# First layer's weights converted two row blocks at a time, with the hand-written order of the first units rearranged

## The chip, the cores and the metric

The kernel runs on one core of a Trainium2 chip. The metric is device time in microseconds (us) of one execution. The engines are PE (matrix multiply), DVE (vector), ACT (scalar activation), POOL (GpSimd) and SP, which only issues transfers here.

## The reference

Sparse attention (a local window of 96 keys and 8 global keys, a bias per head), a feed-forward layer with softmax-weighted units and a layer norm, then a gated feed-forward layer. All is float32; the weights come as 8-byte numbers.

```python
# attention: B, H, S, D = 2, 8, 768, 64
scores = scale * (q @ k.T) + bias            # bias: -slope[h] * distance
scores = where(is_global | is_local, scores, -1e9)
a = exp(scores - max); a = a / (sum(a) + 1e-9)
x = (a @ v) as (1536, 512)
# first layer: w_in 512 x 1024, w_out 1024 x 512
h = x @ w_in
solu = h * softmax(h)
ln = (solu - mean) / sqrt(var + 1e-6) * g_ln
x = ln @ w_out
# second layer: w_gate, w_val 512 x 1536, w_out 1536 x 512
xn = x / rms(x) * rms_g
out = (silu(xn @ w_gate) * (xn @ w_val)) @ w_out
```

## The kernel before

**Units.** The 1536 tokens are 12 units of 128 rows. Units 0 and 1 are the first row blocks of the two batch entries and see 128 keys; the others see 256. A unit's attention is done in halves of four heads: `s_mm` (scores, PE), `s_max` (bias and row maximum, DVE, L278 to L282), `s_exp` (ACT, L289), `s_norm` (reciprocal on DVE, L297 and L298, then four multiplications on POOL, L300), `t_mm` (transposes, PE, L316), `t_evac` (copy out of PSUM, ACT L324 or DVE L326), `attend` (PE, L338). `x_hi` and `x_lo` split the result into two parts for PE (L218 on ACT, L356 on DVE).

**First layer.** `up_mm u half` multiplies x by half of w_in (12 matrix multiplies of 512 columns, L473): eight with the high part of the weights, `win0`, and then four with the low part, `win1`. `up_max`, `so_exp`, `so_mul`, `so_mean`, `so_var` make the softmax-weighted layer norm (DVE and ACT). A PSUM tile `hp` of `up_mm` is free for a later unit when `so_mul` (L505) has read it; there are two such buffers. `ln_t` transposes, `down` multiplies by w_out (L558).

**The weights.** A number of 8 bytes lies in memory as a low and a high word. For each block of 128 rows of w_in or w_out and 512 columns there is a load of 512 KB (`w_load`), a scaled copy of the high word (`w_scale`, one instruction, mostly on ACT), three bit operations on DVE (`w_bits` 0, 1, 2 at L390, L392, L396), the rounded high part (`w_hi`, mostly ACT) and the low part, the difference (`w_lo`: L453 on POOL for w_in, L456 on DVE for w_out). There are 16 blocks: 0 to 3 are the first half of w_in, 4 to 7 the second, 8 to 15 are w_out. The staging tiles `wsh` and `wsl` hold two blocks each, the converted words `wch` and `wcl` four each; a load waits until its place has been converted.

**What sets the order.** The string `START` is a list of steps, read from left to right. Each step puts its instructions at the end of its engine's queue, and each engine works through its queue in order, waiting where data are missing. `START` covers units 0 to 3 wholly, the attention of unit 4, most of that of unit 5, and all 16 weight blocks; its first two lines before the change are

```python
load_n, n_floats, load_qk 0 0, load_qk 0 1, bias_tile 0, bias_tile 1
bias_heads 0 0 4 scalar, bias_heads 0 4 8 gpsimd, s_mm 0 0, s_max 0 0, w_load 0, s_mm 0 1 h
```

Behind it the units 4 to 11 run in a loop (`slot`) in which PE's order is written out and the other engines are ordered by a scheduler; then comes the second layer.

Of the kernel before, what the change touches and what calls it, by code (L numbers as in the profile page):

```python
# [51 lines left out]
t_evac 0 1 1, w_scale 3 scalar, w_hi 1 scalar, w_bits 2 1, t_mm 0 2, w_bits 3 0
t_evac 0 2 1, attend 0 0, t_mm 0 3, t_evac 0 3 1, w_load 4, attend 0 1
w_lo 0 gpsimd, w_load 5, w_bits 2 2, w_hi 2 scalar, w_load 6, attend 0 3
s_max 1 0, attend 0 2, w_bits 3 1, w_lo 1 gpsimd, x_hi 0 scalar, x_lo 0
w_bits 3 2, s_exp 1 0, w_hi 3 scalar, w_lo 2 gpsimd, late_constants, w_load 7
w_scale 4 vector, s_max 1 1, w_bits 4 0, w_lo 3 gpsimd, s_norm 1 0, w_bits 4 1
w_scale 5 scalar, s_exp 1 1, w_scale 6 scalar, up_mm 0 0 d, t_mm 1 1, load_qk 3 0
load_v 1, t_mm 1 0, load_v 2, w_scale 7 scalar, t_evac 1 0 1, w_bits 5 0
w_bits 4 2, w_bits 5 1, bias_heads 1 4 6 scalar, w_hi 4 scalar, t_evac 1 1 1, bias_heads 1 0 2 gpsimd  # L60
w_bits 6 0, bias_heads 1 6 8 scalar, s_norm 1 1, s_mm 2 0, w_bits 7 0, t_mm 1 2
t_evac 1 2 1, w_bits 6 1, attend 1 0, w_bits 5 2, w_bits 7 1, t_mm 1 3
attend 1 1, w_hi 5 scalar, t_evac 1 3 1, w_bits 6 2, w_load 9, w_bits 7 2
w_hi 6 scalar, w_lo 4 gpsimd, s_max 2 0, attend 1 2, up_max 0 0, attend 1 3
w_hi 7 scalar, w_load 8, w_scale 8 vector, load_v 4, s_mm 2 1, w_lo 5 vector
s_exp 2 0, x_hi 1 scalar, w_load 10, s_max 2 1, w_load 11, w_lo 6 gpsimd
w_lo 7 gpsimd, w_scale 9, load_qk 4 0, s_norm 2 0, s_exp 2 1, x_lo 1
w_bits 9 0, up_mm 0 1, load_qk 3 1, up_max 0 1, w_bits 8 0, so_exp 0
w_bits 9 1, s_norm 2 1, so_mul 0 0, w_mul 8 none, w_scale 10 scalar, so_mul 0 1
t_mm 2 0, w_bits 8 1, up_mm 1 0, so_mean 0, w_bits 9 2, w_bits 8 2  # L70
up_max 1 0, load_qk 4 1, t_mm 2 1, up_mm 1 1, t_mm 2 2, up_max 1 1
t_evac 2 1 1, t_evac 2 0 1, w_load 12, so_var 0, w_hi 9 scalar, s_mm 3 0
t_evac 2 2 1, attend 2 0, attend 2 2, w_hi 8 scalar, attend 2 1, so_exp 1
t_mm 2 3, w_mul 11 none, s_max 3 0, s_mm 3 1, w_bits 10 0, s_exp 3 0
w_lo 9 vector, t_evac 2 3 0, attend 2 3, x_hi 2 scalar, w_mul 15 none, w_scale 12 gpsimd
so_mul 1 1, s_norm 3 0, s_max 3 1, w_scale 11 scalar, load_v 3, s_exp 3 1
x_lo 2, t_mm 3 0, w_bits 11 0, so_mul 1 0, w_bits 12 0, so_mean 1
w_mul 9 none, t_mm 3 1, w_bits 10 1, s_norm 3 1, w_bits 10 2, so_var 1
t_evac 3 0 1, up_mm 2 0, w_load 14, w_hi 10 scalar, t_evac 3 1 1, up_mm 2 1
# [990 lines left out]
```

## Time and profile before

| | |
|---|---|
| three runs | 558.94, 559.98, 561.72 us (median 559.98) |
| the profiled execution, its own time | 558.16 us |
| its span, first to last instruction | 556.3 us |
| steps of START | up to about 93 us |
| one unit of the loop behind it | 18.9 us |

The span and the time of the profiled execution differ by 1.9 us, which lie ahead of the first and behind the last instruction. A timeline row gives start and duration; where instructions overlap in an engine's pipeline, the distance between the starts of two neighbours is what one of them costs in a full queue, and that is less than its duration.

### The profile page before, as it was taken

The page shows a single profiled execution, that of the slowest core. Times are in us where ns is not written, and L with a number is a line of the kernel's source. Part 1 is how long each engine was busy: PE and PEld are TensorE (multiplying, and loading weights), DVE is VectorE, ACT ScalarE, POOL GpSimd, SP SyncE. Part 2 cuts the span into 40 slices and gives each one's busy share as a digit, 9 for nine tenths or more (in the row PEclk, how much of TensorE's full clock was granted, in tenths as well). Part 3 has the DMA queues.
Part 4 walks back from the last instruction along what each step waited for, and adds up shares of the span by engine and source line. Part 5 has one row for each costly group of instructions (what it writes and reads, how often), then busy time and mean ns, then how long its engine had stood idle before and what let it go on. Part 6 is the DMA issues. An engine that isn't in the chain of part 4 may idle for free.

```text
span 556.3 us, 7639 instructions
## 1 busy us (share of the span) xinstructions
PE 527.8 (95%) x2736; PEld 424.1 (76%) x2736; DVE 333.4 (60%) x797; ACT 236.6 (43%) x557; POOL 179.0 (32%) x207
## 2 busy tenths in 40 slices
...
GB/s 290 254 240 142 247 31 67 95 95 47 51 94 39 1 76 77 115 113 16 140 148 151 1 0 1 75 151 1 1 0 1 75 151 77 0 77 0 77 0 82
DMA packets 16670, 45.93 MB, mean 83 GB/s; under 512 B 1904, under 2 KB 2928, under 8 KB 16624
## 3 DMA queue, kind: packets, MB, share of 16 engines
...
## 4 chain that ended last, share of the span: by engine, by line
PE 70%; DVE 20%; POOL 4%; ACT 3%; issue 2%; DMA 1%; POOLq 0%; DVEq 0%; ACTq 0%; SPq 0%
PE gv L628 30%; PE op L652 15%; PE yp L558 11%; PE hp L473 8%; DVE p L278 3%; DVE e L505 2%; POOL p L300 2%; PE tp L316 2%; DVE hst L481 2%; DVE wc L392 1%; PE xps L338 1%; DVE wc L390 1%; DVE xlo L356 1%; PE tp L587 1%; DVE llo L224 1%
## 5 line engine op out<-in xcount | busy, mean ns | idle before, releaser
L628 PE MATMUL gv<-xgh,w2hi 128*128 128x512 f32 x288 | 112.2, 390 | 0.0
L628 PE MATMUL gv<-xgl,w2hi 128*128 128x512 f32 x288 | 112.0, 389 | 0.0
L628 PE MATMUL gv<-xgh,w2lo 128*128 128x512 f32 x288 | 112.0, 389 | 0.0
L224 POOL TENSOR_TENSOR alo<-th,ahi 128x512 fp32r<-128x512 f32 x36 | 47.6, 1322 | 169.9 <-ACT ahi L223 169.8
L300 POOL TENSOR_SCALAR p<-p,ast 128x256 f32<-128x256 f32 (+1 forms) x96 | 56.7, 608 | 103.5 <-DVE ast L282 67.5
L615 DVE SCALAR_TENSOR_TENSOR th<-th,gv 128x512 f32<-128x512 f32 x36 | 24.7, 685 | 100.0 <-ACT th L614 99.9
L224 POOL TENSOR_TENSOR w2lo<-wc,w2hi 128x512 fp32r<-128x512 f32 x36 | 49.0, 1366 | 63.3 <-ACT w2hi L223 63.3
L473 PE MATMUL hp<-win,xhi 128*128 128x512 f32 x192 | 66.0, 407 | 0.7 <-ACT xhi L218 0.7
L628 PEld LDWEIGHTS gv<-xgh,w2lo 128*128 128x128 f32 x288 | 54.1, 188 | 11.3
L628 PEld LDWEIGHTS gv<-xgl,w2hi 128*128 128x128 f32 x288 | 54.1, 188 | 11.2
L628 PEld LDWEIGHTS gv<-xgh,w2hi 128*128 128x128 f32 x288 | 54.1, 188 | 11.0
L558 PE MATMUL yp<-wout,lhi 128*128 128x512 f32 x192 | 60.9, 398 | 0.3 <-DVE wout L456 0.3
L652 PE MATMUL op<-w2hi,alo 128*128 128x512 f32 x144 | 56.4, 392 | 2.3 <-POOL alo L224 2.3
L223 ACT ACTIVATE ahi<-th 128x512 fp32r<-128x512 f32 x36 | 22.7, 631 | 82.7 <-DVE th L616 82.7
L652 PE MATMUL op<-w2hi,ahi 128*128 128x512 f32 x144 | 56.2, 391 | 1.4 <-ACT ahi L223 1.4
L614 ACT ACTIVATE th<-gv 128x512 f32<-128x512 f32 x36 | 21.3, 591 | 82.1 <-PE gv L628 82.1
L652 PE MATMUL op<-w2lo,ahi 128*128 128x512 f32 x144 | 56.1, 389 | 0.0
L289 ACT ACTIVATE p<-p,ast 128x256 f32<-128x256 f32 (+1 forms) x96 | 45.9, 480 | 7.2 <-DVE ast L282 4.0
L473 PEld LDWEIGHTS hp<-win,xhi 128*128 128x128 f32 x192 | 37.1, 193 | 9.1 <-ACT xhi L218 1.4
L616 DVE SCALAR_TENSOR_TENSOR th<-th,gv 128x512 f32<-128x512 f32 x36 | 24.6, 684 | 30.1 <-PE gv L628 29.9
L558 PEld LDWEIGHTS yp<-wout,lhi 128*128 128x128 f32 x192 | 34.9, 188 | 7.3 <-DVE wout L456 0.8
L473 PE MATMUL hp<-win,xlo 128*128 128x512 f32 x96 | 38.7, 403 | 0.4 <-DVE xlo L356 0.4
...
## 6 DMA issues: line engine op xcount, KB each, us to landing
...
```

The source lines that it names most:

```text
L223: self.nc.scalar.activation(out=hi, in_=src, func=AF.Copy)
L224: lo_eng.tensor_tensor(lo, src, f32(hi), ALU.subtract)
L278: nc.vector.tensor_tensor_reduce(pt[:, i, 0:W], sp[h2][:, pl, :], bias[:, 4 * hh + i, :], 1.0, -3.0e38, ALU.add, ALU.max, st[:, 0, i:i + 1],)
L289: self.nc.scalar.activation(out=pt[:, i, 0:W], in_=pt[:, i, 0:W], func=AF.Exp, scale=0.125, bias=st[:, 1, i:i + 1], accum_out=st[:, 2, i:i ...
L300: nc.gpsimd.tensor_scalar(pt[:, i, 0:W], pt[:, i, 0:W], st[:, 3, i:i + 1], 0.0, ALU.mult, ALU.add)
L473: nc.tensor.matmul(hp, a[:, k, :], self.win[w][:, k, c], start=(n == 0), stop=(n == len(mms) - 1))
L558: nc.tensor.matmul(yp, a[:, k, :], self.wout[w][:, k, :], start=(k == 0 and n == 0), stop=(k == KF - 1 and n == 2),)
L614: nc.scalar.activation(out=a, in_=g, func=AF.Tanh, scale=0.5)
L615: nc.vector.scalar_tensor_tensor(out=a, in0=a, scalar=1.0, in1=g, op0=ALU.add, op1=ALU.mult)
L616: nc.vector.scalar_tensor_tensor(out=a, in0=a, scalar=0.5, in1=v, op0=ALU.mult, op1=ALU.mult)
L628: nc.tensor.matmul(pp, w[:, c], a[:, k, :], start=(n == 0), stop=(n == 3 * KD - 1))
L652: nc.tensor.matmul(self.ops[t], a[:, c], w[:, c0], start=(first and n == 0), stop=(last and n == 2))
```

## The change

Row blocks are loaded and converted in pairs. There are 8 pairs: 0 and 1 are the first half of w_in, 2 and 3 the second, 4 to 7 are w_out. A load is 1 MB; `w_scale` and the three `w_bits` work on 1024 columns instead of 512; `w_hi` and `w_lo` of w_in take 1024 columns in one instruction, except that `w_lo` on POOL, and both for w_out, are two instructions of 512. A pair fills a whole staging tile. `START` is written anew. In it the bias of heads 4 to 7 of the first kind and of heads 0 and 1 of the second moves from POOL to ACT; `w_lo` of pairs 0, 1 and 3 is on DVE, that of pair 2 on POOL; every `w_scale` and `w_hi` is on ACT; the normalisation of unit 3's second half and `x_hi 4` are on DVE; `t_evac 1 1` is on DVE.

```diff
 START = """\
-bias_heads 0 0 4 scalar, bias_heads 0 4 8 gpsimd, s_mm 0 0, s_max 0 0, w_load 0, s_mm 0 1 h
...
+load_n, n_floats, load_qk 0 0, load_qk 0 1, bias_tile 0, bias_tile 1, bias_heads 0 0 4 scalar, s_mm 0 0
...
-    def s_norm(self, u, hh):
+    def s_norm(self, u, hh, eng="gpsimd"):
...
         for i in range(4):
-            nc.gpsimd.tensor_scalar(
-                pt[:, i, 0:W], pt[:, i, 0:W], st[:, 3, i:i + 1], 0.0, ALU.mult, ALU.add
-            )
+            self.scaled(eng, pt[:, i, 0:W], pt[:, i, 0:W], st[:, 3, i:i + 1])
...
     def w_load(self, n):
...
+        st, w = self.early
+        i = self.n_early
+        self.n_early += 1
+        st, w = st[i % 2], w[i % 4 // 2][:, 2 * (i % 2):2 * (i % 2) + 2]
+        half, k = divmod(2 * n, KD) if n < KD else (0, 2 * (n - KD))
+        name = "w_in" if n < KD else "w_out"
+        src = self.d[name][k * P:(k + 2) * P, 2 * half * CW:2 * (half + 1) * CW]
+        self.nc.sync.dma_start(
+            out=st.rearrange("p a b c -> p a (b c)"), in_=src.rearrange("(a p) f -> p a f", p=P)
+        )
+        self.w1[n] = st, w
...
     def w_hi(self, n, eng="scalar"):
...
+        if n < KD:
+            half, k = divmod(2 * n, KD)
+            out = [t[:, k:k + 2, half * CW:half * CW + CW] for t in self.win]
+            self.scaled(eng, out[0], w, 1.0)
         else:
...
+            for i in range(2):
+                self.scaled(eng, out[0][:, i], w[:, i], self.gln[:, k + i:k + i + 1])
...
     def w_lo(self, n, eng="gpsimd"):
...
+        if n < KD and eng == "vector":
+            self.nc.vector.tensor_tensor(lo, w, f32(hi), ALU.subtract)
+            return
+        for i in range(2):
+            if n < KD:
+                self.nc.gpsimd.tensor_tensor(lo[:, i], w[:, i], f32(hi[:, i]), ALU.subtract)
```

Three places in the queues, with the changed kernel's own line numbers in its rows. The first is DVE's queue around the `x_lo` of unit 0, without which PE can't go beyond the first multiply of `up_mm 0 0`. Before (L392 and L396 are the bit operations of single blocks):

```order
L282 TENSOR_SCALAR ast<-ast 128x4
L392 SCALAR_TENSOR_TENSOR wch<-wsl,wch 128x512
L356 TENSOR_TENSOR xlo<-xps,xhi 128x512
L396 SCALAR_TENSOR_TENSOR wch<-wsl,wch 128x512
L157 MEMSET neghalf 128x1
```

The same place now; L370 and L374 are the bit operations of pair 1, L423 is `w_lo 0`, L334 is `x_lo 0`:

```order
L262 TENSOR_SCALAR ast<-ast 128x4
L135 MEMSET neghalf 128x1
L370 SCALAR_TENSOR_TENSOR wch<-wsl,wch 128x1024
L423 TENSOR_TENSOR win_131<-wch,win_130 128x2x512
L374 SCALAR_TENSOR_TENSOR wch<-wsl,wch 128x1024
L334 TENSOR_TENSOR xlo<-xps,xhi 128x512
```

Between the row maximum of unit 1's first half and `x_lo 0` there stand three instructions of 1024 columns where there was one of 512; the difference `w_lo 0` was on POOL.

The second place is DVE's queue around the reciprocal of unit 4's second half (the second pair of L297 and L298), on which POOL's normalisation and then PE's transposes wait. Before:

```order
L297 TENSOR_SCALAR ast<-ast 128x4
L298 RECIPROCAL ast<-ast 128x4
L481 TENSOR_REDUCE hst<-hp 128x1
L390 TENSOR_SCALAR wcl<-wcl 128x512 x3
L456 SCALAR_TENSOR_TENSOR wout_133<-wch,gln,wout_132 128x512
L481 TENSOR_REDUCE hst<-hp 128x1
L392 SCALAR_TENSOR_TENSOR wcl<-wsl,wcl 128x512
L297 TENSOR_SCALAR ast<-ast 128x4
L298 RECIPROCAL ast<-ast 128x4
L392 SCALAR_TENSOR_TENSOR wcl<-wsl,wcl 128x512
L396 SCALAR_TENSOR_TENSOR wcl<-wsl,wcl 128x512
```

Now (L277 and L278 are the reciprocal, L368 to L374 bit operations, L430 `w_lo 5`, L258 the row maximum of unit 5's first half, which goes on for seven more rows):

```order
L277 TENSOR_SCALAR ast<-ast 128x4
L278 RECIPROCAL ast<-ast 128x4
L456 TENSOR_REDUCE hst<-hp 128x1
L368 TENSOR_SCALAR wcl<-wcl 128x1024 x2
L430 SCALAR_TENSOR_TENSOR wout_133<-wch,gln,wout_132 128x512 x2
L456 TENSOR_REDUCE hst<-hp 128x1
L370 SCALAR_TENSOR_TENSOR wcl<-wsl,wcl 128x1024
L277 TENSOR_SCALAR ast<-ast 128x4
L278 RECIPROCAL ast<-ast 128x4
L374 SCALAR_TENSOR_TENSOR wcl<-wsl,wcl 128x1024
L470 TENSOR_SCALAR hst<-hst 128x1
L258 ISA p,ast<-sA,bias_144 128x256
```

The row maximum of unit 5 has moved up to right behind one bit operation after the reciprocal; before, it stood behind four more weight instructions, two `w_lo` and the six of `check_n`.

The third place is PE's queue at the end of `START`: `up_mm 4 1` (hp) with the last multiplies by the low part of w_out (`wout_133`) in it. Before:

```order
L473 MATMUL hp<-win_130,xhi 128x512
L473 MATMUL hp<-win_130,xlo 128x512
L558 MATMUL yp<-wout_133,lhi 128x512
L558 MATMUL yp<-wout_132,llo 128x512
L473 MATMUL hp<-win_130,xhi 128x512
```

Now:

```order
L448 MATMUL hp<-win_131,xhi 128x512 x3
L533 MATMUL yp<-wout_133,lhi 128x512
L533 MATMUL yp<-wout_132,llo 128x512
L533 MATMUL yp<-wout_132,lhi 128x512
L533 MATMUL yp<-wout_133,lhi 128x512
L533 MATMUL yp<-wout_132,llo 128x512
L448 MATMUL hp<-win_131,xhi 128x512
```

Five multiplies of `down 0 3` instead of two are left for this place, and they stand behind eleven of the twelve multiplies of `up_mm 4 1` instead of behind four.

## Rows read from the trace of the kernel before

**Rows 1.** The page: busy time, share of the span, instructions of each engine.
```profile
PE 527.8 (95%) x2736; PEld 424.1 (76%) x2736; DVE 333.4 (60%) x797; ACT 236.6 (43%) x557; POOL 179.0 (32%) x207
```

**Rows 2.** Busy time by stretch: PE, PEld, DVE, ACT, POOL; then PEclk, DMA share, GB/s.
```profile
7.28:36.60 29.32, 21.76 (x93) 13.19 (x93) 26.02 (x85) 21.29 (x68) 23.58 (x27) 0.88 0.75 255
36.60:92.30 55.70, 51.89 (x342) 39.69 (x342) 53.33 (x172) 42.32 (x113) 22.70 (x33) 1.00 0.46 157
0.00:100.00 100.00, 83.43 (x518) 60.68 (x520) 89.63 (x295) 71.14 (x198) 50.84 (x76) 0.97 0.54 181
106.94:125.84 18.90, 18.76 (x125) 15.06 (x124) 12.34 (x44) 10.56 (x30) 4.81 (x10) 1.00 0.23 70
```

**Rows 3.** What PE waited for from 7 to 102 us.
```profile
PE tp L316 <- POOL p L300: 7.9, 11, 1.8
```

**Rows 4.** Busy time in 0 to 100 us of L390, L392, L396, L282, in turn.
```profile
0.00:100.00 100.00, 6.99 (x16) 0.97 0.54 181
0.00:100.00 100.00, 11.61 (x16) 0.97 0.54 181
0.00:100.00 100.00, 11.93 (x16) 0.97 0.54 181
0.00:100.00 100.00, 4.34 (x13) 0.97 0.54 181
```

**Rows 5.** POOL's busy time in 0 to 100 us, L220 first, then L453 (DVE first).
```profile
0.00:100.00 100.00, 1.23 (x3) 7.68 (x8) 0.97 0.54 181
0.00:100.00 100.00, 0.68 (x1) 9.85 (x7) 0.97 0.54 181
```

**Rows 6.** Timeline of DVE: start, duration; the spacing of starts is the cost.
```profile
48.32 0.08 DVE L278 DVE_READ_ACCUMULATOR2_ANT ast<- 128x1 f32 x1
48.66 0.08 DVE L278 DVE_READ_ACCUMULATOR2_ANT ast<- 128x1 f32 x1
...
49.55 0.42 DVE L390 TENSOR_SCALAR wch<-wch 128x512 uint32<-128x512 uint32 x1
49.88 0.74 DVE L456 SCALAR_TENSOR_TENSOR wout<-wch,gln,wout 128x512 fp32r<-128x512 f32 x1
...
62.39 0.68 DVE L396 SCALAR_TENSOR_TENSOR wch<-wsl,wch 128x512 uint32<-128x512 uint32 x1
62.99 0.68 DVE L392 SCALAR_TENSOR_TENSOR wcl<-wsh,wcl 128x512 uint32<-128x512 uint32 x1
...
85.24 0.75 DVE L514 TENSOR_SCALAR e<-e,hst 128x1024 f32<-128x1024 f32 x1
85.91 0.16 DVE L297 TENSOR_SCALAR ast<-ast 128x4 f32<-128x4 f32 x1
```

**Rows 7.** Timeline of POOL: four normalisations of 256 columns each row.
```profile
52.43 1.84 POOL L300 TENSOR_SCALAR p<-p,ast 128x256 f32<-128x256 f32 x4 [1.94 <-DVE ast L298]
...
75.11 4.01 POOL L300 TENSOR_SCALAR p<-p,ast 128x256 f32<-128x256 f32 x4 [1.34 <-DVE ast L298]
```

**Rows 8.** Timeline of PE at the places that the steps speak of.
```profile
20.47 0.80 PE L473 MATMUL hp<-win,xlo 128*128 128x512 f32 x1
...
36.53 0.50 PE L473 MATMUL hp<-win,xhi 128*128 128x512 f32 x1
...
40.13 0.48 PE L473 MATMUL hp<-win,xhi 128*128 128x512 f32 x1
...
52.96 1.80 PE L316 MATMUL tp<-ident,p 128*128 128x128 f32 x8 [1.02 <-POOL p L300]
...
78.70 1.35 PE L316 MATMUL tp<-ident,p 128*128 128x128 f32 x8 [1.42 <-POOL p L300]
...
94.19 1.09 PE L338 MATMUL xps<-pT,v 128*64 128x128 f32 x16
...
100.95 0.66 PE L587 MATMUL tp<-ident,xn 128*128 128x128 f32 x4 [0.47 <-DVE llo L224]
```

**Rows 9.** PE's clock (the column PEclk) in one stretch, as in rows 2.
```profile
29.30:36.04 6.74, 5.97 (x34) 3.61 (x32) 5.86 (x15) 5.57 (x17) 5.79 (x8) 0.50 0.31 103
```

More of the change, by code (lines that the diff above doesn't have):

```diff
@@ L52 @@
[L52 to L79, printed above, removed]
@@ L80 @@
-w_lo 8 vector, load_qk 5 0, w_mul 13 none, up_max 2 0, t_mm 3 3, t_mm 3 2
-up_max 2 1, t_evac 3 3 1, s_mm 4 0, t_evac 3 2 1, w_bits 11 1, w_mul 10 none
-so_exp 2, attend 3 0, attend 3 2, w_lo 10 vector, attend 3 3, w_bits 11 2
-w_bits 12 1, attend 3 1, s_max 4 0, load_qk 5 1, so_mul 2 1, ln_t 0 0
-x_hi 3 scalar, x_lo 3, w_load 13, ln_t 0 1, w_hi 11 scalar, w_load 15
-w_scale 15 gpsimd, so_mul 2 0, s_mm 4 1, s_max 4 1, w_bits 12 2, s_exp 4 0
-up_mm 3 0, s_norm 4 0, w_scale 13 scalar, up_mm 3 1, up_max 3 0, t_mm 4 0
@@ L87 @@
-w_scale 14 scalar, w_bits 14 0, s_exp 4 1, w_bits 13 0, t_evac 4 0 1, w_bits 15 0
-s_mm 5 0, w_lo 11 vector, up_max 3 1, attend 4 0, t_mm 4 1, w_hi 12 scalar
-w_bits 13 1, s_norm 4 1, down 0 0, w_bits 15 1, t_evac 4 1 1, w_bits 13 2
-w_hi 13 scalar, so_exp 3, attend 4 1, w_bits 15 2, load_v 5, t_mm 4 3
-t_mm 4 2, down 0 1, t_evac 4 2 1, attend 4 2, w_bits 14 1, w_lo 12 vector
-t_evac 4 3 1, w_hi 15 scalar, check_n, s_max 5 0, w_bits 14 2, attend 4 3
-s_mm 5 1, x_hi 4 scalar, w_lo 13 vector, w_hi 14 scalar, x_lo 4, so_mul 3 1
@@ new lines @@
+s_exp 2 0, s_norm 2 0, up_mm 0 1, s_exp 2 1, up_max 0 1, x_lo 1, so_exp 0, w_bits 4 0, s_norm 2 1
+so_mul 0 0, so_mul 0 1, t_mm 2 0, w_bits 4 1, so_mean 0, up_mm 1 0, w_bits 4 2, up_max 1 0, t_mm 2 1
+up_mm 1 1, t_mm 2 2, load_qk 4 1, t_evac 2 0 1, so_var 0, t_evac 2 1 1, s_mm 3 0, up_max 1 1, t_evac 2 2 1
+attend 2 0, load_qk 3 1, attend 2 2, attend 2 1, w_hi 4 scalar, t_mm 2 3, so_exp 1, s_mm 3 1, s_max 3 0
+t_evac 2 3 0, s_exp 3 0, attend 2 3, so_mul 1 1, s_norm 3 0, s_max 3 1, w_scale 5 scalar, load_v 3
```

90 lines of the change are left out of this document (40 added, 50 removed).

## The prediction

> **What bounds the kernel now.** The page comes first: PE is busy for 95% of the span, DVE for 60% [rows 1]. The share of PE is an average over two regimes, so the next view is the busy time by stretch. In the loop behind `START` a unit takes 18.90 us, and PE is busy for 18.76 of them, DVE for 12.34 [rows 2]: there PE is the bound, and a gain on DVE, ACT or POOL is worth nothing. In `START` it is otherwise. From 36.6 to 92.3 us DVE is busy for 53.33 of 55.70 us and PE idle for 3.81; from 7.3 to 36.6 us PE is idle for 7.56 [rows 2]. The list of PE's waits says for what: 7.9 us in 11 waits for POOL's normalisation ahead of the transposes [rows 3]. POOL is slow there because of DVE: four normalisations take 1.84 us beside a row maximum, and 4.01 us beside bit operations [rows 7]. So the change can only act by when PE gets through `START`. All that PE is early or late at `up_mm 4`, some 90 us in, goes to the end unchanged, as the loop has 0.14 us of slack a unit. The most to be had behind 36.6 us is the 3.8 us of PE's idle time there.
>
> **What one wide instruction costs.** The spacing of starts in DVE's full queue is read from [rows 6]. A `tensor_scalar` of 512 columns costs 0.33 us (49.55 to 49.88), one of 1024 columns 0.67 (85.24 to 85.91). A two-input operation of 512 columns costs 0.60 (62.39 to 62.99), a step of the row maximum of 256 columns 0.34 (48.32 to 48.66). So 256 columns more cost 0.26, and the trace has no two-input operation of 1024 columns; I take 0.60 + 2 x 0.26 = 1.12 us. The bounds are 1.20 (twice the narrow one, nothing saved) and 0.67 (if it went like the wide `tensor_scalar`); the two-input rows are the nearer.
>
> **The sum on DVE.** Bits: 16 x (0.33 + 2 x 0.60) = 24.5 us become 8 x (0.67 + 2 x 1.12) = 23.3, so -1.2. Three copies (`w_hi 0`, `w_scale` 4 and 8) leave DVE [rows 5]: -1.0. `w_lo`: three of 1.12 for one of 0.60, +2.8. `t_evac 1 1` of 256 columns +0.3, `x_hi 4` +0.6, four normalisations of 256 columns at half of 0.33 +0.7. Together **+2.2 us**: joining the blocks saves less than what is moved to DVE costs.
>
> Against it stands what POOL no longer takes. Of L220 all 7.68 us go; of L453 9.85 us stay two of seven, so -7.0 [rows 5]; one set of normalisations goes, between 1.84 and 4.01, say 2.5 [rows 7]. That is 17.2 of POOL's 50.84 us [rows 2]. What POOL's presence costs DVE now is the excess of durations over undisturbed ones (0.42 for L390, 0.68 for L392 and L396, 0.16 for four columns [rows 6]): 6.99 - 16 x 0.42 = 0.3; 11.61 + 11.93 - 32 x 0.68 = 1.8; 4.34 - 13 x 0.16 = 2.3 [rows 4]; in all 4.4 us. If a third of it goes with a third of POOL's work: **-1.5 us**. The bounds are 0 (what goes lay where DVE wasn't full) and -4.4. DVE's sum is +0.7, between -2.2 and +2.2.
>
> **Where it meets PE**, followed along the queues with these costs.
>
> *The first unit.* `x_lo 0` now stands behind three instructions of 1.12 us where one of 0.60 stood. It ends at about 21.8 us, and the second multiply of `up_mm 0 0`, now at 20.47 [rows 8], comes 1.3 us later. Further on there is a gain: POOL no longer makes two heads of bias between the normalisations of unit 1, so `s_mm 2 1`, right ahead of `up_mm 0 1`, comes 1.8 us earlier. But the last two multiplies of `up_mm 0 1` need `w_lo 3`, now on DVE behind two row maxima (4 x 0.34 + 0.2 each [rows 6]), till about 37.6; and `x_lo 1` follows it. `up_mm 1 0` starts at 39.9 for 40.13 [rows 8]: **-0.2**. ACT, 71% busy over `START` [rows 2], takes the bias heads, which delays `w_scale 3` but not this chain. SP issues fewer, longer loads; pair 0 is first needed after the first exponentials, by which time its two blocks have landed today as well, so the transfers cost nothing unless a load of 1 MB lands a microsecond later than two halves.
>
> *The middle.* From `s_mm 3 0` to the transposes at 52.96 [rows 8] the chain is row maximum, exponentials, reciprocal, normalisation, and none of it changes: PE's 1.02 us of waiting stays. The few tenths gained are lost again at `x_hi 3`, which now stands on ACT behind two `w_hi` of 512 columns. Zero, give or take 0.5.
>
> *Unit 4.* Between the two reciprocals stand 2 x 0.67 + 2 x 0.66 + 1.12 = 3.8 us of weight work instead of 3 x 0.33 + 0.66 + 0.60 = 2.3, and one operation of 0.60 ahead of the first has gone; the second comes at about 75.6, 0.6 later. POOL then waits out one bit operation of 1.12 us, and runs beside the row maximum of unit 5, at 1.84 / 4 = 0.46 us each [rows 7]: 75.8 + 1.1 + 1.8 = 78.7 instead of 79.1. The transposes end at 78.9, not 79.8: **-0.9**, of the 1.42 us of waiting at 78.70 [rows 8].
>
> *The end of START.* DVE has 17.3 us of work from that reciprocal to the end of `w_lo 7`, where it had 16.6 to the end of the last block. `so_mul 3 0`, which frees the buffer for `up_mm 4 1`, comes at 90.1, so PE, there at 89.1, waits 1.0; then it reaches the late multiplies of `down 0 3` as `w_lo 7` is done (92.3 and 92.9). The attention of unit 5 starts at 94.05 for 94.19 [rows 8]: the 0.9 is given back, **+0.8**. `t_evac 5 3`, behind DVE's longer queue, takes up to 0.3 more ahead of 100.95.
>
> Sum: -0.2 + 0.1 - 0.9 + 0.8 + 0.2 = 0.0 us. On the profiled execution of 558.16 us that is 558.2. The median of the runs is 1.8 us higher, at 559.98; against it I forecast **559.9 us, no change**. What a measurement of this kernel can tell from no change is about 0.5%, 2.8 us.
>
> **The rivals.**
>
> *Faster: POOL's absence is worth more.* If most of the 4.4 us goes, or a two-input operation of 1024 columns is nearer to 0.67, DVE is 2 to 4 us ahead at 90 us, `so_mul 3 0` and `w_lo 7` wait for nobody, and PE keeps the 0.9 and most of the waits at 52.96 and 78.70: -3.5, **556.5 us**. For it: 17 us of POOL gone, two waits of PE that hang on POOL [rows 3]. Against it: the wait at 52.96 is a chain through ACT that the change leaves alone. Chance 0.25.
>
> *Slower: wide bit operations hold POOL back.* Beside operations of 0.60 a normalisation took 1.00 us [rows 7], that is 0.46 and most of a DVE instruction. Beside 1.12 it would take 1.5. It decides at unit 4: if the scores of unit 5 are not there when DVE comes to their row maximum, or POOL falls behind it, all four take 6.0 instead of 4.0, and the transposes end 2.2 later; the same in units 0 and 2 adds 1: +3.2, **563 us**, chance 0.12. The Trainium skill, SBUF — State Buffer, section "Who interferes with whom", says that VectorE in a two-port mode or with two SBUF inputs locks out a GpSimd instruction that reads SBUF for the whole instruction, which speaks against this change. By that rule a normalisation beside a bit operation would be 0.46 + 0.60 = 1.06, which the row's 1.00 bears out, and with one SBUF input, as in the row maximum, nothing, which the 1.84 bears out.
>
> *Slower: the clock.* From 29.30 to 36.04 us PE ran at 0.50 of the granted clock, the 1.2 GHz level [rows 9]; then at 1.00 to the end of `START` [rows 2]. It rose behind a stretch in which PE was busy for 5.97 of 6.74 us. The new order puts gaps of one to two microseconds there (for `x_lo 0`, for pair 3, for `w_lo 3`). If it stays low over `up_mm 0 1` and `1 0`, the 3.6 us from 36.53 to 40.13 [rows 8] count twice; up to 38.2 that is hidden behind `w_lo 3`, and from 44 on it costs 3 us. **563 us**, chance 0.06.
>
> **How the numbers follow.** No change has 0.57; its own range, from the sum's +-2 and the scatter of the three runs, is 557.5 to 562. From 556.5 to 562.8 all but some 0.2 are held. Faster by over 0.5% is the first rival, 0.25; slower the other two, 0.18.
>
> **What would show it.** In the changed profile: two-input operations of 1024 columns spaced at 1.1 us; DVE's busy time up to 100 us within 1.5 of 89.6; POOL's down from 50.8 to 34; PE's second multiply 1 us later than 20.47; the wait near 78.7 halved; a new wait of PE on `so_mul` or `w_lo` near 90; the transposes of xn near 101. I am wrong if `up_mm 1 0` starts more than 2 us off 40.1, if the transposes of unit 4 move by more than 2 us, or if PE's clock rises at another time.

## The result, and the profile after

The changed kernel takes 565.11 us (median of 10 runs, 561.27 to 566.17), the kernel before 559.54 (10 runs, 558.07 to 562.55). The ratio is 1.0089, 95% interval 1.0062 to 1.0116: slower, by 5.6 us between the medians and 5.0 by the ratio, and outside the range that was forecast. The profiled execution took 565.0 us, its span is 563.2.

Busy time of the changed kernel by the stretches of [rows 2] (PE, PEld, DVE, ACT, POOL, granted clock, DMA share, GB/s):

```profile
7.28:36.60 29.32, 19.57 (x91) 12.84 (x92) 24.54 (x72) 20.86 (x59) 12.04 (x18) 0.94 0.74 270
36.60:92.30 55.70, 51.70 (x321) 38.54 (x319) 48.89 (x147) 39.14 (x105) 12.89 (x20) 0.94 0.42 149
0.00:100.00 100.00, 80.62 (x465) 58.56 (x466) 83.55 (x252) 67.06 (x184) 29.39 (x57) 0.95 0.50 177
```

DVE is no longer full: from 36.6 us it is idle for 6.8 us instead of 2.4. PE's clock is 0.94 where it was 1.00. The longer loads cost nothing: no engine waits for a weight block in `START`. PE's rows at the places of [rows 8], of the changed kernel (start, length, and in brackets the wait before and who ended it):

```profile
22.09 0.79 PE L448 MATMUL hp<-win,xlo 128*128 128x512 f32 x1 [1.59 <-DVE xlo L334]
22.68 0.63 PE L448 MATMUL hp<-win,xhi 128*128 128x512 f32 x1
23.11 0.63 PE L448 MATMUL hp<-win,xlo 128*128 128x512 f32 x1
23.53 0.63 PE L448 MATMUL hp<-win,xhi 128*128 128x512 f32 x1
...
35.66 0.70 PE L243 MATMUL sA<-qk 64*128 64x256 f32 x2 [1.95 <-DVE ast L258]
...
37.06 0.64 PE L448 MATMUL hp<-win,xhi 128*128 128x512 f32 x1
37.50 0.63 PE L448 MATMUL hp<-win,xlo 128*128 128x512 f32 x1
...
55.82 1.80 PE L294 MATMUL tp<-ident,p 128*128 128x128 f32 x8 [1.58 <-POOL p L198]
...
64.56 1.03 PE L294 MATMUL tp<-ident,p 128*128 128x128 f32 x8
...
82.50 1.80 PE L294 MATMUL tp<-ident,p 128*128 128x128 f32 x8 [0.22 <-POOL p L198]
...
106.42 0.66 PE L562 MATMUL tp<-ident,xn 128*128 128x128 f32 x4 [0.15 <-DVE llo L204]
```

The reader is to see three things. The transposes of xn stand at 106.42 us for 100.95: `START` lost 5.5 us, and that reaches the end. A wait has appeared that had no row before, 1.95 us at `s_mm 2 1` (35.66), for DVE's row maximum: `s_mm 2 1` needs the two score banks, and `s_max 2 0`, which frees them, stands on DVE behind the bits of pair 3. And behind that wait the multiplies of `up_mm 0 1` stand 0.43 us apart, where two rows further down the wait of 1.58 us leads to the same: nearly twice the 0.23 us of a full clock.

The column of the granted clock does not show every stretch at the lower level. The multiplies of `up_mm 0 0` from 22.68 us on stand 0.43 us apart too, and the column has 1.00 there:

```profile
22.00:24.00 2.00, 1.91 (x5) 1.53 (x6) 1.93 (x13) 2.00 (x5) 1.51 (x4) 1.00 0.52 159
```

So where the column and the spacing of multiplies differ, the spacing counts. DVE's rows ahead of that wait show what lengthened it (L370 and L374 are the bits of pair 3, L258 is `s_max 2 0`), and POOL's row beside them is `w_lo 2`:

```profile
30.56 1.22 DVE L370 SCALAR_TENSOR_TENSOR wcl<-wsl,wcl 128x1024 uint32<-128x1024 uint32 x1
...
32.30 2.27 DVE L374 SCALAR_TENSOR_TENSOR wcl<-wsl,wcl 128x1024 uint32<-128x1024 uint32 x1
34.50 0.41 DVE L258 CUSTOM_DVE_ANT_0 p<-sA,bias 128x256 f32<-128x256 f32 x1
```

```profile
32.23 3.48 POOL L427 TENSOR_TENSOR win<-wcl,win 128x512 fp32r<-128x512 f32 x2 [2.25 <-ACT win L196]
```

The theory from here on: **the loss is the order in `START` together with the clock**. Waits of PE that the new order has, or has longer, bring its clock down to the 1.2 GHz level, and what PE then loses nothing hides. The rivals: **width** (wide bit operations hold POOL back), **engines** (the work moved to DVE), and the waits by themselves, without the clock.

### The profile page after: what moved, and what is told of

Its sections match the earlier page's. It is cut to its first block, busy times and chain, and to the rows that moved or that the text cites. A ratio compares the mean times of both kernels' runs of the same rounds, so it can differ in the third digit from the quotient of the medians.

```text
span 563.2 us, 7589 instructions
## 1 busy us (share of the span) xinstructions
PE 532.2 (94%) x2736; PEld 427.3 (76%) x2736; DVE 334.2 (59%) x778; ACT 237.3 (42%) x554; POOL 158.7 (28%) x190
## 4 chain that ended last, share of the span: by engine, by line
PE 65%; DVE 22%; ACT 6%; issue 3%; POOL 2%; DMA 2%; DVEq 0%; POOLq 0%; ACTq 0%; SPq 0%
PE gv L602 26%; PE op L626 14%; PE yp L533 11%; PE hp L448 9%; DVE p L258 2%; DVE wc L370 2%; DVE wc L374 2%; PE tp L294 2%; DVE wc L368 2%; DVE e L480 2%; DVE hst L456 1%; DMA ws<-in_w 1%; ACT wc L196 1%; PE tp L562 1%; ACT e L473 1%
## 5 line engine op out<-in xcount | busy, mean ns | idle before, releaser
L198 POOL TENSOR_SCALAR p<-p,ast 128x256 f32<-128x256 f32 (+1 forms) x92 | 50.2, 566 | 145.8 <-DVE ast L278 69.9
L448 PE MATMUL hp<-win,xhi 128*128 128x512 f32 x192 | 68.2, 418 | 1.8 <-ACT xhi L196 1.6
L448 PEld LDWEIGHTS hp<-win,xhi 128*128 128x128 f32 x192 | 38.5, 201 | 11.4 <-ACT xhi L196 2.4
L448 PE MATMUL hp<-win,xlo 128*128 128x512 f32 x96 | 40.7, 424 | 2.5 <-DVE xlo L334 2.5
```

Source lines behind the costliest of these rows:

```text
L198: self.nc.gpsimd.tensor_scalar(out, src, scale, 0.0, ALU.mult, ALU.add)
L448: nc.tensor.matmul(hp, a[:, k, :], self.win[w][:, k, c], start=(n == 0), stop=(n == len(mms) - 1))
```

## The experiments

Each is timed against the kernel before on its own chip; where a median is set beside 565.11, the other is that of the kernel changed here.

### Width and engines

`e3_narrow` makes every wide instruction of the conversion as two:

```diff
     def w_scale(self, n, eng="scalar"):
-        self.cv_scale(self.w1[n], eng)
+        st, w = self.w1[n]
+        for i in range(2):
+            self.cv_scale((st[:, i], w[:, i]), eng)
...
```

> The changed kernel with the same order, engines and loads, but each instruction of 1024 columns of the conversion made as two of 512 (scale, bit operations, w_hi, w_lo on DVE). Theory 1 (order and clock): two narrow ones cost 0.08 us more than a wide one, the waits of PE stay where they are: 565 to 567 us. Theory 2 (a wide bit operation holds POOL back for its whole length): POOL's normalisations beside bit operations fall from 2.8 us to about 2, the transposes behind them come earlier, 562 us or less.

Measured: 565.65 us, ratio 1.0126 (1.0105 to 1.0147). Nothing is gained. Two of POOL's normalisations, of the changed kernel and then of this one: the first of unit 0, beside the bits of pair 0, and that of unit 4's second half, at which the rival was to decide:

```profile
10.68 2.81 POOL L198 TENSOR_SCALAR p<-p,ast 128x128 f32<-128x128 f32 x4 [8.39 <-DVE ast L278]
...
81.18 2.63 POOL L198 TENSOR_SCALAR p<-p,ast 128x256 f32<-128x256 f32 x4 [1.87 <-DVE ast L278]
```

```profile
10.99 3.80 POOL L198 TENSOR_SCALAR p<-p,ast 128x128 f32<-128x128 f32 x4 [8.70 <-ACT wch L196]
...
81.60 2.61 POOL L198 TENSOR_SCALAR p<-p,ast 128x256 f32<-128x256 f32 x4 [2.82 <-DVE ast L278]
```

Beside narrow bit operations some take longer and some shorter, the first ten 24.3 us together for 23.3, and at unit 4 there is no difference. The rival of width falls.

`e6_engines` puts the work that was moved in `START` back; only the steps that change are listed, without their neighbours:

```diff
-bias_heads 0 4 8 scalar, w_lo 0 vector, w_lo 1 vector, w_lo 3 vector, w_scale 4, t_evac 1 1 0
+bias_heads 0 4 8 gpsimd, w_lo 0 gpsimd, w_lo 1 gpsimd, w_lo 3 gpsimd, w_scale 4 vector, t_evac 1 1 1
-bias_heads 1 0 2 scalar, s_norm 3 1 vector, x_hi 4 vector
+bias_heads 1 0 2 gpsimd, s_norm 3 1, x_hi 4 scalar
```

> The changed kernel (565.1 us) with its pairs and its order, but the engines of the kernel before: w_lo 0, 1 and 3, two groups of bias heads and the normalisation 3 1 on POOL again, x_hi 4 and t_evac 1 1 on ACT, w_scale 4 on DVE. Theory 3 (the work moved to DVE is the loss): DVE has 4.5 us less to do, PE comes 1 to 2 us earlier, 563 to 564 us. Theory 1 (order and clock; POOL's operations beside wide bit operations only make both longer): the waits of PE stay or grow, bit operations beside w_lo take up to 2.3 us for 1.2, 566 to 569 us.

Measured: 565.92 us, ratio 1.0096 (1.0062 to 1.0130). Its rows of PE:

```profile
28.27 0.50 PE L450 MATMUL hp<-win,xhi 128*128 128x512 f32 x1 [1.71 <-POOL win L429]
...
36.95 0.79 PE L245 MATMUL sA<-qk 64*128 64x256 f32 x1 [2.75 <-DVE ast L260]
```

A new wait for `w_lo` on POOL, and the wait at `s_mm 2 1` is longer. Taking the work off DVE does not help, so the moves to DVE are not the loss by themselves; what they cost or give beside the new waits for POOL is not separated.

### The wait at `s_mm 2 1`

`e1_smax_first` moves one step, `e4_wlo2_dve` takes away what runs beside the slow bit operation:

```diff
-up_max 0 0, w_bits 3 2, s_max 2 0
+up_max 0 0, s_max 2 0, w_bits 3 2
```

```diff
-w_lo 2 gpsimd, load_v 4, s_mm 2 1, x_hi 1 scalar, s_max 2 1, w_load 5, w_lo 3 vector
+load_v 4, s_mm 2 1, x_hi 1 scalar, s_max 2 1, w_load 5, w_lo 2 vector, w_lo 3 vector
```

> The changed kernel (565.1 us) with one step moved: s_max 2 0 stands ahead of w_bits 3 2 on DVE, not behind it. Theory 1 (a PSUM wait in the order, then the clock): s_max 2 0 starts at about 32.3 us for 34.50, PE's wait of 1.95 us ahead of s_mm 2 1 falls below 0.5, up_mm 0 1 starts at about 35.3 for 37.06, and with no gap there its multiplies stand 0.23 us apart, not 0.43; 562 to 563.5 us. Theory 2 (the wide instructions as such, wherever they stand): nothing is gained, 565 us. Theory 3 (DVE's amount of work and the moves between engines): also 565 us, since no work is taken away.

> The changed kernel with w_lo 2 taken from POOL and given to DVE, ahead of w_lo 3. In the changed kernel w_bits 3 2 takes 2.27 us beside POOL's w_lo 2, where others of its kind take 1.22. If that contention makes the wait ahead of s_mm 2 1: w_bits 3 2 takes 1.22, s_max 2 0 starts at 33.45 for 34.50, PE's wait is 0.9 for 1.95, 563 to 564.5 us. If DVE's amount of work is the loss: 1.1 us more of it stands ahead of x_lo 1, up_mm 1 0's second multiply comes 1 us later, 566 us.

Measured: `e1_smax_first` 564.27 us, 1.0095 (1.0065 to 1.0125); `e4_wlo2_dve` 563.79, 1.0102 (1.0064 to 1.0141), with runs from 560.83 to 568.64. In the first, `s_mm 2 1` did come 1.9 us earlier and `up_mm 0 1` began at a full clock, as theory 1 had it, but its rows of PE show where the gain went:

```profile
33.76 0.70 PE L245 MATMUL sA<-qk 64*128 64x256 f32 x2 [0.46 <-DVE ast L260]
...
37.40 0.51 PE L450 MATMUL hp<-win,xhi 128*128 128x512 f32 x1 [1.04 <-ACT win L198]
...
41.98 1.14 PE L296 MATMUL tp<-ident,p 128*128 128x128 f32 x4 [2.23 <-POOL p L200]
```

`w_bits 3 2`, now behind `s_max 2 0`, releases `w_hi 3` on ACT later; behind `w_hi 3` stand the exponentials of unit 2, and PE waits 2.23 us for their normalisation, with multiplies 0.43 us apart behind that wait instead (43.35 and 43.78 us). The wait can be moved along the chain through ACT, DVE and POOL, but one step doesn't remove it. `e4_wlo2_dve` in its profile had the bit operation at 1.21 us, the wait at 0.73 and the clock at 1.00 over 36 to 45 us, and the low clock only behind the wait of unit 3 (1.59 us): the contention is a part, as expected, but its scatter is too wide to put a number to it.

### The clock

`e2_fill` leaves the order alone and gives PE multiplies whose products are overwritten, at its two longest waits behind 30 us:

```diff
+    def dummy(self, out, n):
+        for _ in range(n):
+            w = self.win[0][:, 0]
+            self.nc.tensor.matmul(out, w[:, 0:P], w[:, 0:512], start=True, stop=True)
...
-s_mm 2 1
+fill 0 1 6, s_mm 2 1
...
-t_mm 3 0
+t_mm 3 0 6
```

> The changed kernel with twelve multiplies that compute nothing needed: six into the accumulator of up_mm 0 1 ahead of s_mm 2 1, six into the transposes' PSUM tile ahead of t_mm 3 0, in the two places where PE waits 1.95 and 1.58 us and runs at the 1.2 GHz level behind it. No wait of PE is taken away. Theory 1 (the clock is most of the loss): the multiplies of up_mm 0 1 and up_mm 2 0 stand 0.23 us apart for 0.43, up_mm 1 0 and all behind it comes 1.5 to 2 us earlier, unit 3 another 1.5: 561 to 562.5 us. Rival (the gaps themselves are the loss and the low clock is covered by the chain through DVE and ACT): 565 us, or 566 if the extra multiplies end after the wait.

Measured: 561.84 us, ratio 1.0042 (1.0020 to 1.0065), 3.3 us less than 565.11 and 2.6 less by the two ratios, with their intervals some 0.7 to 4.6. So useless work at the waits gave back about half of the loss. Its profile has the clock column at 1.00 in all of `START`, though the last four multiplies of `up_mm 0 0` take 1.91 us there too, and shows a second difference:

```profile
32.50 1.22 DVE L378 SCALAR_TENSOR_TENSOR wcl<-wsl,wcl 128x1024 uint32<-128x1024 uint32 x1
```

```profile
33.13 1.66 PE L448 MATMUL hp<-win 128*128 128x512 f32 x6
34.81 0.70 PE L245 MATMUL sA<-qk 64*128 64x256 f32 x2
...
103.43 0.66 PE L579 MATMUL tp<-ident,xn 128*128 128x128 f32 x4
```

The last bit operation of pair 3, which began before the first filling multiply, took 1.22 us for 2.27, and `s_mm 2 1` came 0.85 us earlier. Of the 3.0 us at xn's transposes (103.43 for 106.42) that much is not the filling. The next run, `e5_x_hi3`, has the same filling and one more edit, and shows its effect side by side with the changed kernel, since its PE came to the wait at the same moment:

```diff
-w_hi 5 scalar, x_hi 3 scalar
+x_hi 3 scalar, w_hi 5 scalar
```

> The kernel with the twelve filling multiplies (561.8 us, its clock at 1.00 through all of START), and x_hi 3 moved ahead of w_hi 5 on ACT. There PE waits 0.73 us for x_hi 3 and 0.23 for x_lo 3 at up_mm 3 0. If that order is part of what the clock leaves over (2.5 us at the transposes of xn, 103.43 against 100.95): both waits go, down 0 0 comes 0.9 us earlier than 76.04, 561 us. If DVE, which is behind by then, sets unit 4 whatever PE does: the wait ahead of the transposes at 79.50 grows by what is saved, 561.8 us.

```profile
33.67 1.72 PE L448 MATMUL hp<-win 128*128 128x512 f32 x6
35.66 0.70 PE L245 MATMUL sA<-qk 64*128 64x256 f32 x2 [0.27 <-DVE ast L260]
...
37.06 0.50 PE L465 MATMUL hp<-win,xhi 128*128 128x512 f32 x1
37.40 0.39 PE L465 MATMUL hp<-win,xlo 128*128 128x512 f32 x1
37.63 0.40 PE L465 MATMUL hp<-win,xhi 128*128 128x512 f32 x1
...
61.83 1.03 PE L298 MATMUL tp<-ident,p 128*128 128x128 f32 x8
```

`s_mm 2 1` at 35.66 and `up_mm 0 1` at 37.06, to the hundredth as in the changed kernel, but with six multiplies in the gap, and behind them 0.23 us from one to the next instead of 0.43. The transposes behind unit 2's first-layer multiplies stand at 61.83 us for 64.56. These 2.7 us are the clock's part by itself up to there, with two gaps filled and the one edit of the order still to come. The edit of unit 3 gave nothing: 561.68 us, 1.0039 (1.0016 to 1.0062). The wait for `x_hi 3` is gone, but at unit 4 (80.70 us) PE waits 1.73 us where it was 0.79 in `e2_fill`, as the second expectation had it.

`e12_after_fill2` was meant for the second layer: nine such multiplies ahead of its first output multiplies, `START` untouched.

```diff
             for n, (a, w) in enumerate(((hi, wh), (hi, wl), (lo, wh))):
+                if (sw, g, t) == (0, 0, 0) and first and n != 1:
+                    for _ in range(5 - n // 2):
+                        nc.tensor.matmul(self.ops[1], wh[:, 0:P], wh[:, 0:512], start=True, stop=True)
```

> The changed kernel with the nine multiplies in the second layer's first wait alone; START is untouched. In its profile the clock was 0.86 over 300 to 312 us and the next 12 multiplies took 3.6 us for 2.0. If the filling holds it: 563.5 us, 1.6 less than 565.1. If the clock there depends on something else than that wait: 565 us.

Measured: 566.25 us (560.98 to 567.29), no gain. The row of the first five of the nine shows why the run says nothing of that wait:

```profile
262.06 1.30 PE L628 MATMUL op<-w2hi 128*128 128x512 f32 x5
```

They stand some 35 us ahead of the wait that they were meant for, at a place where PE had none, and only add nine times 0.23 us, some 2 us. The same holds for the nine in `e10_all` and `e11_before_fill2` and for eleven, some 2.5 us, in `e13_all_fills` and `e14_end`.

But the execution that was profiled, at 560.98, is the best witness of this study: the same `START`, and from 26 us on its multiplies stay at a full clock. Its rows of PE, DVE and POOL, in three fences:

```profile
33.73 0.70 PE L243 MATMUL sA<-qk 64*128 64x256 f32 x2 [0.76 <-DVE ast L258]
...
35.13 0.50 PE L448 MATMUL hp<-win,xhi 128*128 128x512 f32 x1
35.47 0.39 PE L448 MATMUL hp<-win,xlo 128*128 128x512 f32 x1
...
52.78 1.80 PE L294 MATMUL tp<-ident,p 128*128 128x128 f32 x8 [1.58 <-POOL p L198]
...
78.22 1.80 PE L294 MATMUL tp<-ident,p 128*128 128x128 f32 x8 [0.54 <-POOL p L198]
...
102.13 0.66 PE L562 MATMUL tp<-ident,xn 128*128 128x128 f32 x4
```

```profile
31.43 1.21 DVE L374 SCALAR_TENSOR_TENSOR wcl<-wsl,wcl 128x1024 uint32<-128x1024 uint32 x1
32.56 0.42 DVE L258 CUSTOM_DVE_ANT_0 p<-sA,bias 128x256 f32<-128x256 f32 x1
```

```profile
31.70 3.31 POOL L427 TENSOR_TENSOR win<-wcl,win 128x512 fp32r<-128x512 f32 x2 [0.20 <-ACT win L196]
```

Over 30 to 36, 36 to 45 and 54 to 64 us, first the changed kernel, then this one:

```profile
30.00:36.00 6.00, 4.05 (x26) 2.53 (x24) 5.93 (x13) 3.92 (x9) 3.48 (x2) 0.72 0.55 198
36.00:45.00 9.00, 8.29 (x34) 6.29 (x33) 6.44 (x22) 6.94 (x23) 2.65 (x6) 0.81 0.72 272
54.00:64.00 10.00, 8.36 (x36) 6.09 (x31) 8.55 (x30) 6.25 (x18) 1.85 (x4) 0.83 0.62 238
```

```profile
30.00:36.00 6.00, 5.24 (x39) 3.43 (x39) 5.96 (x17) 5.18 (x10) 4.81 (x4) 1.00 0.68 249
36.00:45.00 9.00, 8.57 (x39) 6.06 (x38) 8.32 (x22) 5.56 (x20) 4.65 (x8) 1.00 0.61 239
54.00:64.00 10.00, 9.99 (x77) 8.11 (x76) 9.69 (x26) 6.37 (x18) 0.09 (x1) 1.00 0.56 205
```

The transposes of xn stand at 102.13 us for 106.42: 4.3 us between two executions of one instruction order. How it grows can be followed. In the changed kernel's profile the last four multiplies of `up_mm 0 0` still ran slowly (1.91 us from 25.24 on, for 1.13), so the transposes behind them and `t_evac 1 0` on ACT came 0.77 us later (27.69 for 26.92), and with it `w_scale 3` and the bits of pair 3. These then met `w_lo 2` on the wrong side: a bit operation that began 0.07 us behind POOL's took 2.27 us, one that began 0.27 us ahead of it 1.21. `s_mm 2 1` came 1.93 us later, 0.87 of it brought along and 1.06 from the longer bit operation; its gap was longer, and the low clock followed. Behind the fall over 37 to 41 us the lag is 3.04 us (55.82 for 52.78), behind the one over 58 to 61 us 4.65 (64.56 for 59.91), and unit 4 gives 0.4 back. So of the 4.3 us some 2.4 come behind the two falls and 1.9 ahead of them.

Other profiles agree: from `s_mm 2 1` to xn's transposes it takes 70.8 us in the changed kernel and 68.4, 68.6 and 68.9 in `e12_after_fill2`, `e2_fill` and `e13_all_fills`, which have multiplies at a full clock from there on. And over all executions of one kernel the short ones have the higher mean clock: of the ten of the changed kernel one has 0.993 and 561.27 us, the others 0.981 to 0.988 and 563.86 to 566.17; of the seven of `e12_after_fill2` three have 0.991 to 0.996 and 560.98 to 564.38 us, four 0.979 to 0.987 and 566.25 to 567.29.

`e8_before` asks the same of the kernel before, `e7_before_fill` fills its waits in unit 1, and `e11_before_fill2` has the nine lines of `e12_after_fill2`.

```diff
-t_mm 1 1
+t_mm 1 1 8
...
-t_mm 1 2
+t_mm 1 2 3
```

> The kernel before as it is, for the granted clock of each of its executions and a second profile. In the profile of the changed kernel the clock falls to 0.86 over 300 to 312 us, behind the wait of the second layer's first output multiplies; in that of the kernel before it stays at 1.00 there, behind a wait of the same length. If the changed order causes that, every run of the kernel before has 0.990 or more; if it comes and goes, some runs have 0.987 and are 1.6 us longer.

> The kernel before (559.5 us) with eleven filling multiplies of 256 columns in two places where PE waits for POOL in unit 1 (1.75 and 0.79 us at 27.29, 0.77 at 31.41), ahead of and in its stretch at the 1.2 GHz level from 29.30 to 36.04. If that stretch costs time: the transposes, scores and attention of unit 1 and 2 go at twice the speed, up_mm 0 1 starts 1 to 2 us earlier than 36.53, 557.5 to 558.5 us. If the chain through DVE and POOL sets that start: 559.5 us.

> The kernel before with the nine multiplies in the second layer's first wait alone. If the clock falls behind that wait in part of its executions, all of them have 0.99 or more and the median comes down by up to 1.5 us, 558 to 558.5 us; if it hardly does, 559.5 us.

Measured: 558.44 us for the unchanged kernel (0.9952 to 1.0005); 560.36, 1.0017 (0.9992 to 1.0043), and 559.94, 1.0021 (1.0004 to 1.0037), for the two filled ones: no gain from either. `e7_before_fill` does not decide what the slow stretch costs: in its profile the clock over 30 to 36 us is 0.50 as before, and the first multiplies of `up_mm 0 1` start no earlier (36.81 us). `e8_before` does. In the second profile of the kernel before, the clock over 30 to 36 us was 0.84, for 0.50 in [rows 9]. Its rows of PE:

```profile
34.88 0.50 PE L473 MATMUL hp<-win,xhi 128*128 128x512 f32 x1
...
39.84 0.44 PE L316 MATMUL tp<-ident,p 128*128 128x128 f32 x2 [1.58 <-POOL p L300]
...
101.49 0.66 PE L587 MATMUL tp<-ident,xn 128*128 128x128 f32 x4 [0.47 <-DVE llo L224]
```

`up_mm 0 1` starts 1.65 us earlier than in [rows 8], waits 1.58 us for POOL, and all behind is as late as ever: 101.49 against 100.95. In the kernel before a slow clock over 30 to 36 us is covered by the normalisation that PE would wait for anyway. In the changed one it is not. In that second profile the clock was also at 0.94 over 300 to 312 us, where the changed kernel has 0.86 and the first profile of before 1.00: the loss in the second layer (1.6 us in the changed kernel's profile) comes with either order. What a filling in that wait would do stays open. The nine multiplies of `e11_before_fill2`, at 260.91 us, are only more work: the third output multiply behind that wait came at 299.60 us for 297.36.

`e13_all_fills` has `e2_fill`'s filling, two more in `START` and eleven multiplies in the second layer, with no edit of the order. The two new ones:

```diff
-up_mm 0 0 d
+fill 0 1 6, up_mm 0 0 d
...
-t_mm 1 2
+t_mm 1 2 6
...
```

> The changed kernel, its order untouched, with filling multiplies in every wait of PE of over 1.3 us from 19 us on: six ahead of up_mm 0 0, six of 256 columns ahead of t_mm 1 2, and those ahead of s_mm 2 1, of t_mm 3 0 and of the second layer's first output. If the falls of the clock are most of the loss in every execution, and no order or engine has to be changed for it: the clock is at 0.993 or more in nearly all runs, the profile of START lies within 0.5 us of the one execution that ran at 1.00 throughout (transposes of xn at 102.13), 560 to 561 us and little scatter. If that one execution owed its time to something else: 562 to 565 us as before.

Measured: 567.45 us, ratio 1.0141 (1.0112 to 1.0171). The expectation failed. `up_mm 0 0` ran at a full clock, but over 30 to 36 us the clock was at 0.50 all the same, and there six filling multiplies ahead of `s_mm 2 1` take longer than in `e5_x_hi3` (1.72), with PE no longer waiting for anything but them:

```profile
35.59 2.11 PE L448 MATMUL hp<-win 128*128 128x512 f32 x6
37.63 0.48 PE L245 MATMUL sA<-qk 64*128 64x256 f32 x1
...
266.46 1.52 PE L646 MATMUL op<-w2hi 128*128 128x512 f32 x6
```

`s_mm 2 1` comes at 37.63 us for 35.66, the clock holds behind it, and the transposes of xn are as late as in the changed kernel (106.52 us for 106.42). So filling helps where PE waits at a clock that the filling can hold, and is in the way where the clock is low when it begins. The 2.3 us beyond 565.11 are about what the eleven multiplies at 266 us add.

### The rest

What the clock leaves over is 1.1 to 2.4 us: xn's transposes stand at 102.13 us in `e12_after_fill2` and at 103.43 in `e2_fill`, against 101.03 in `e11_before_fill2`, whose `START` is that of the kernel before. Three runs looked for it on DVE. `e9_unit4` (561.7 us without its edit) takes a wide scale on ACT and, on DVE, a wide shift, a wide two-input operation and a row maximum of the first layer out of the way of unit 4's second reciprocal:

```diff
-w_scale 6 scalar, up_max 3 0, up_mm 3 1, w_bits 6 0, t_mm 4 0, w_bits 7 0
-s_mm 5 0, s_exp 4 1, t_evac 4 0 1, w_lo 5 vector, up_max 3 1
+up_max 3 0, up_mm 3 1, t_mm 4 0, w_bits 7 0, s_mm 5 0, s_exp 4 1, w_scale 6 scalar
+t_evac 4 0 1, w_lo 5 vector, s_norm 4 1, w_bits 6 0, up_max 3 1
...
-s_norm 4 1, w_bits 6 2
+w_bits 6 2
```

> The kernel with the filling multiplies and x_hi 3 ahead of w_hi 5 (561.7 us), and in unit 4: w_scale 6 behind s_exp 4 1 on ACT, and on DVE s_norm 4 1 ahead of w_bits 6 0 and up_max 3 1. There PE, 0.9 us earlier at up_mm 3 0, waited 1.73 us more for POOL's normalisation at 80.70, whose reciprocal stood on DVE behind two wide shifts that waited 1.01 us for the wide w_scale 6. If that chain (a pair scaled as a whole, then its bits, ahead of the reciprocal) is what the clock leaves over: the reciprocal comes at about 75 us for 79.00, the wait is gone, the transposes of xn come at about 102.5 us for 104.64, 559.5 to 560 us. If the time only moves on to the weights of the last two pairs (w_lo 6, w_lo 7 later by 2 us): PE waits there instead, 561.7 us.

Measured: 562.01 us, 1.0048 (1.0026 to 1.0071). The reciprocal came at 74.92 us for 79.00 and the wait fell from 1.73 to 0.41, but PE then waited 1.01 us for an evacuation on ACT (row at 82.23), and xn's transposes stand at 103.27 for 104.64, of which 0.8 us were there at `s_mm 2 1` already (34.85 for 35.66): the wait moved on, if not to the weights.

`e10_all` adds to `e9_unit4` the nine multiplies in the second layer and a new order of the first unit (`w_lo 0` behind `x_lo 0`, `s_norm 1 1`, two bias heads, `w_scale 3` and `s_max 2 0` earlier), `e14_end` has all of the fillings of `e13_all_fills`, the edits of units 3 and 4, and `ln_t 1 0`, `ln_t 1 1` ahead of `s_max 5 1`:

```diff
-w_lo 0 vector, load_v 2, x_hi 0 scalar, w_bits 1 2, s_exp 1 0, w_hi 1 scalar, w_load 3, x_lo 0
+load_v 2, x_hi 0 scalar, w_bits 1 2, s_exp 1 0, w_hi 1 scalar, w_load 3, x_lo 0, w_lo 0 vector
...
-w_bits 2 0, w_bits 2 1, bias_heads 1 4 6 scalar, w_bits 2 2
+w_bits 2 0, s_norm 1 1 gpsimd, w_bits 2 1, bias_heads 1 0 2 scalar, w_scale 3 scalar
...
-w_bits 3 1, w_hi 2 scalar
+s_max 2 0, w_bits 3 1, w_hi 2 scalar
```

```diff
-s_max 5 1, ln_t 1 0, ln_t 1 1, so_mul 3 0
+ln_t 1 0, ln_t 1 1, s_max 5 1, so_mul 3 0
```

> The last kernel, and also: w_lo 0 behind x_lo 0; s_norm 1 1 ahead of w_bits 2 1; the bias heads 1 0 2 and w_scale 3 earlier on ACT; s_mm 2 0 ahead of attend 1 0, s_max 2 0 ahead of w_bits 3 1; and nine multiplies that compute nothing needed in the second layer's first wait for ahi and alo. If PE's waits of the first unit are lost time: the second multiply of up_mm 0 0 at about 20.9 for 22.09, up_mm 0 1 one to two us earlier, 556.5 to 558.5 us, with the clock at 1.00 over 300 to 312 us. If DVE's chain from unit 2 on sets the pace whatever the first unit does: only the second layer's part, 559 us.

> The last kernel with the edits of unit 3 and 4 (x_hi 3 ahead of w_hi 5, w_scale 6 behind s_exp 4 1, s_norm 4 1 ahead of w_bits 6 0), and with the evacuations ln_t 1 0 and 1 1 ahead of s_max 5 1 on DVE, where PE waits 0.26 us at up_mm 4 0 and 0.43 for a bank at the transposes of unit 5. If the order of DVE around 87 us is the 1.2 us that stay at a full clock: up_mm 4 1 comes 0.5 to 1 us earlier than 91.13, 559 to 560 us. If s_max 5 1, 1.2 us later, delays unit 5's second half by as much: as the last kernel, or 0.5 more.

Measured: 565.51 us, 1.0119 (1.0100 to 1.0139), and 566.94, 1.0139 (1.0113 to 1.0165). Without the 2.0 and 2.5 us of the multiplies in the second layer both would, by estimate, still be above the 562.01 of `e9_unit4`. In `e10_all` the second multiply came at 21.11 us, but PE then waited 2.22 us at 42.15 for unit 2's normalisation, as in `e1_smax_first`, with the low clock behind it. In `e14_end` PE waits 1.46 us for `so_mul 3 0` at `up_mm 4 1` (94.89). None of the kernels tried beats the one before.

## Why the prediction was wrong

**What bounds the kernel** was read rightly: what PE loses in `START` reaches the end. It is 5.5 us late at xn's transposes and 5.6 at the second layer's first output multiply (301.30 for 295.73).

**Cost of a wide instruction**, forecast 1.12 us: right. In the changed kernel wide two-input operations start at 19.08 and 20.22, 1.14 apart.

**The sum on DVE**, forecast +0.7 us between -2.2 and +2.2: within its bounds. Up to the transposes of xn DVE is busy for 89.5 us, for 90.6 in the kernel before. The test named for it, 89.6 us within 1.5 by 100 us, was badly chosen: 83.55, because a late kernel has done less by then. What the sum could not see is that DVE now waits: 3.3 us for wide `w_scale` on ACT, 0.2 before, since a pair is scaled as a whole before its first bit operation.

**The first unit**: the second multiply at 21.8 is right (22.09). "`s_mm 2 1` comes 1.8 us earlier" is not: 0.8 us later, or 1.2 earlier in the execution at a full clock. The walk followed its data and not its PSUM banks, which `s_max 2 0` frees from behind the bits of pair 3. `up_mm 1 0` came at 41.86, or 39.47 at a full clock, for a forecast of 39.9.

**The middle**, forecast 0: the wait at `x_hi 3` (71.53 us) is 0.89 us, not a few tenths. **Unit 4**, forecast -0.9: at a full clock the transposes end at 79.78, for 79.80 before, so 0. The wait fell as forecast, but the eight transposes go at POOL's pace, 1.80 us for 1.35 [rows 8]. **The end**, forecast +0.8: from `up_mm 4 0` to attention 5 it takes 8.7 us (86.58 to 95.24) where it took 7.5 (86.67 to 94.19): +1.1.

At a clock that holds, then, the sum of 0.0 stands against a measured +1.1 us in `e12_after_fill2`, within the +-2 that it was given, and +2.4 in `e2_fill`, where `up_mm 0 0` stayed slow to its end.

**The clock** is the step that failed. The sum has no term for it; it stands only as a rival, "chance 0.06", with 3 us if it "stays low over `up_mm 0 1` and `1 0`". One place and the mechanism were right: it fell over 37 to 41 us, behind the new wait at `s_mm 2 1`, and that fall cost 1.1 us, less than priced, as `up_mm 1 0` ran at a full clock. A second fall, over 58 to 61 us, was not foreseen and cost 1.6 us. The chance was far too small. I had taken the clock of one profile of the kernel before (1.00 from 36 us on [rows 2]) for a property of that stretch, and listed the new gaps of one to two microseconds without asking what each would do to it.

The wait at `s_mm 2 1` is the other part. The walk had the score banks wrong, as said, and gave the bit operation ahead of it 1.12 us, where it took 2.27 beside POOL's `w_lo 2`. That and the slow end of `up_mm 0 0` are the 1.9 us that lie ahead of the two falls. Shown: filling two of the gaps gives back 3.3 us, 2.6 by the ratios; from the same moment on, a clock that holds is worth 2.7 us up to the end of unit 2's multiplies (`e5_x_hi3`); one order of instructions differs by 4.3 us between two executions that first differ in the clock of `up_mm 0 0`. Together 4.3 and 1.1 make the 5.4 us between xn's transposes at 106.42 and at 101.03. That the slow end of `up_mm 0 0` caused the longer bit operation is followed in one pair of profiles and not shown beyond it: in `e2_fill` the end was as slow, and the operation took 1.22 us.

**The other slow rival**, that wide bit operations hold POOL back, is refuted by `e3_narrow` and by the changed kernel itself, where unit 4's second four normalisations take 2.63 us, not 6.0. The faster one, that POOL's absence is worth more, did not come about: POOL fell to 29.4 us by 100 us, below the 34 forecast, and DVE did get shorter operations, but waited for others.

**Open** stays what decides whether the clock falls. Behind a wait of 1.58 us at unit 3's transposes it fell in the changed kernel and not in `e12_after_fill2`; filling it in one place held it and in `e13_all_fills` did not. The Trainium skill, TensorE: Matmul & The Clock Gate, Part 1, says that the chip's watch over activity runs on its own and doesn't start with the kernel, so that the point of transition varies from run to run; the two profiles of one order agree with that, and no run here shows more of it. The scatter of the kernel before, 557.4 to 562.6 us over all its runs, was not traced to a place either; in `e8_before` its longest runs, 561.23 and 561.88 us, have the lowest mean clock, 0.982.
